# One transpose of q in place of two, earlier loads of q and k, and PV five steps behind its scores in place of seven

## The chip, the cores and the metric

The kernel runs on one core of a Trainium2 chip. The metric is the device time of one launch in microseconds (us). Each comparison was run in rounds beside the kernel before, on the same chip. A run over 1.5% above the fastest of its kernel counts as slow.

## The reference

Eight batches of eight heads, 576 positions, head size 64; then two matrix products with a leaky ReLU between them.

```python
scores = q @ k.T / 8                                 # per batch and head
thresh = scores.max(-1) - tau
scores = where(scores >= thresh, scores, -1e9)
attn   = softmax(scores)
x      = (attn @ v) -> [4608, 512]                   # heads side by side
h      = x @ w_in                                    # [4608, 2048]
out    = maximum(0.01 * h, h) @ w_out                # [4608, 512]
```

## The kernel before

The kernel is one loop over 144 **steps**, 18 per batch. A step takes 128 rows of q for a pair of heads. It makes scores (`sc`) on TensorE, copies them with their maximum on VectorE (`sf`), subtracts (`P`), and takes the exponential on ScalarE (`w`). Two steps make a **unit** (the last units, in the final batch, have one). A unit's weights `w` are transposed by one DMA into `wt`, and later TensorE multiplies them by v ("PV"). Finished groups of rows give "h units" and "o units" of the two matrix products, one pair of them a step.

For the next batch, each half (two pairs of heads) of k and q is loaded in fp32 (`km`, `qm`), split in two fp16 parts (`ks`, `qs`) on ScalarE and GpSimd, and transposed by DMA (`kst`, `qst`; a **turn** in the code).

SyncE issues, in one in-order queue, all loads of q and k, all transposes and all stores. GpSimd issues the loads of v and of the weights.

```python
LAG = 7                       # steps from a unit's last scores to its PV
PREP = (3, 9)                 # first step of preparing each half of the next batch
...
def turn(nm, b, hb, g=None):  # DMA transposes
    t = turned(nm, b, hb); s_ = split_tile(nm, b, hb)
    if nm == "k":
        nc.sync.dma_start(out=t..., in_=s_..., transpose=True)          # 128 rows
    else:
        nc.sync.dma_start(out=t[:, g]..., in_=s_[ds(64 * g, 64)]..., transpose=True)   # 64 rows
...
for b in range(1, B):
    s0 = 18 * (b - 1)
    for hb in range(2):
        t0 = s0 + (PREP1 if b < 2 else PREP)[hb]
        at(t0 - 4, load k half);  at(t0 - 3, load q half)
        at(t0 - 1, fp16 of k);    at(t0 + 1, fp16 of q)      # ScalarE
        ...
        at(t0 + 4, turn k)
        for g in range(2):
            at(t0 + 7 + g, turn q of pair g)
    for i in range(4):
        at(18 * b + i, load_v(b, i))
```

Units that end in step 130 or later, close to the end, have a lag of four steps in both kernels. Within a step, TensorE's order is scores, then o and h units, then PV. SyncE's order is stores, then the `wt` transpose of the unit that ended two steps earlier, then the loads and turns above.

## Time and profile before

| | before |
|---|---|
| median of three runs | 538.18 us (536.41 to 541.07) |
| profiled span | 537.4 us |
| first `sf` / last step's first `sf` to the end | at 12.8 us / 45.8 us |
| batches 1 to 6, mean of one (from its first `sf` to the next batch's) | 60.8 us |

In the profile PE is TensorE and PEld its weight loads, DVE is VectorE, ACT ScalarE, POOL GpSimd, and SP SyncE (SPq: it issues a DMA). The **granted clock** is the share of TensorE's full clock rate that it got. The profile names a group by line, engine and operation, with "output<-input" by the program's names. The waits view gives total us, how often, and the longest. A batch of 18 undisturbed steps, 3.12 us each by the starts of `sf`, would take 56.2 us.

### The profile page before, as it was taken

The numbers are of one execution on the slowest core, as the hardware profiler recorded it, in microseconds if no ns is written. First come the engines' busy times: TensorE is split into PE (matmuls) and PEld (weight loads), VectorE is DVE, ScalarE is ACT, GpSimd is POOL, SyncE is SP. The second block draws the span as 40 slices with busy tenths as digits, with TensorE's granted clock in tenths as the row PEclk, the third lists the DMA queues.
The fourth block names the chain that finished last, engine by engine and source line by source line (L and its number), as shares of the span: only waits on it lengthen the run. The fifth ranks groups of instructions, "written<-read, shape, count | busy, mean of one in ns | idle before, by whom it ended". The sixth has DMA issues, their size and how long they took to land.

```text
span 537.4 us, 13446 instructions
## 1 busy us (share of the span) xinstructions
PE 476.8 (89%) x4912; PEld 294.3 (55%) x4912; DVE 463.8 (86%) x1213; ACT 421.8 (78%) x924; POOL 278.2 (52%) x476
## 2 busy tenths in 40 slices
PE   5655885999989997999998995999999998999996
PEld 3323553655655664666654663566555665566673
DVE  4976895999999996999997995999999999999542
ACT  6785894998799886898897884898799888778331
POOL 5475843675477634574576643675466643222000
PEclk9758797999999997999998998899999999999999
DMA  8999999999999999999999999999999999976401
GB/s 269 207 189 236 158 183 250 222 189 183 208 221 224 166 195 263 222 176 192 227 184 205 153 199 245 241 189 172 219 199 241 182 166 188 189 125 122 96 25 59
DMA packets 279617, 101.79 MB, mean 189 GB/s; under 512 B 254464, under 2 KB 266752, under 8 KB 279552
## 3 DMA queue, kind: packets, MB, share of 16 engines
q1 hardware_dynamic: 266496, 92.03, 90.9%
q0 software_dynamic: 13056, 8.92, 12.5%
q8 instruction: 38, 0.62, 0.5%
q14 instruction: 27, 0.22, 0.2%
HBM read 36.70 MB, written 9.44 MB: 86 GB/s over the span
## 4 chain that ended last, share of the span: by engine, by line
DVE 41%; PE 15%; issue 15%; DMA 13%; POOL 7%; ACT 6%; SPq 2%; POOLq 0%; DVEq 0%; ACTq 0%
DVE sf L398 16%; DMA km<-in_k_dram 8%; DVE gT L223 7%; DVE P L554 7%; PE op L243 6%; PE hp L243 5%; DMA wt<-w 4%; DVE w L544 4%; POOL P L525 3%; PE sc L338 3%; DVE osb L279 3%; DVE xT L379 2%; SPq L179 2%; ACT P L524 2%; ACT gT L257 1%
## 5 line engine op out<-in xcount | busy, mean ns | idle before, releaser
L398 DVE TENSOR_SCALAR_CACHE_REDUCE sf<-sc 128x576 f32<-128x576 f32 x288 | 205.0, 747 | 8.3 <-PE sc L338 7.5
L559 ACT ACTIVATE w<-P 128x576 f16<-128x576 f16 x288 | 193.7, 674 | 7.9 <-DVE P L554 3.8
L243 PE MATMUL op<-wout,gT 128*128 128x512 f16 x576 | 150.9, 386 | 13.5 <-DVE osb L279 13.1
L243 PE MATMUL hp<-xT,win 128*128 128x256 f16 (+1 forms) x1344 | 153.9, 261 | 5.5 <-DVE gT L223 3.9
L338 PE MATMUL sc<-kst,qst 64*128 64x320 f16 (+1 forms) x1536 | 137.8, 299 | 18.6 <-DVE sf L398 17.8
L243 PEld LDWEIGHTS <-win 128*128 128x128 f16 x1344 | 118.4, 99 | 50.7 <-issue 10.0
L524 ACT ACTIVATE P<-sf,bb 128x576 f16<-128x576 f32 x144 | 111.1, 771 | 43.6 <-POOL bb L523 39.2
L223 DVE SCALAR_TENSOR_TENSOR gT<-hp,gT 128x512 f16<-128x512 f32 x144 | 98.3, 683 | 35.5 <-ACT gT L257 35.5
L338 PEld LDWEIGHTS <-qst 64*128 64x128 f16 x1536 | 75.9, 98 | 70.7 <-issue 51.2
L525 POOL TENSOR_SCALAR P<-sf,bb 128x576 f16<-128x576 f32 x139 | 105.8, 761 | 14.1
L257 ACT ACTIVATE gT<-hp 128x512 f16<-128x512 f32 x144 | 83.6, 580 | 18.9 <-PE hp L243 18.9
L243 PEld LDWEIGHTS <-gT 128*128 128x128 f16 x576 | 46.4, 98 | 76.2 <-issue 40.7
L523 POOL TENSOR_SCALAR bb<-mx 128x2 f32<-128x2 f32 x139 | 27.3, 196 | 107.0 <-DVE sf L398 95.3
L554 DVE TENSOR_SCALAR P<-P 128x1152 int16<-128x1152 int16 x144 | 81.7, 568 | 0.0
L369 PE MATMUL pv<-wt,v 128*64 128x256 f16 (+2 forms) x1000 | 55.9, 251 | 11.5 <-DMA wt<-w 11.0
L559 ACT ACTIVATION_READ_ACCUMULATOR w<-P 128x1 f32 x288 | 54.3, 188 | 0.0
L369 PEld LDWEIGHTS <-v 128*64 128x64 f16 x1000 | 37.6, 111 | 27.6 <-issue 23.6
L149 ACT ACTIVATE ks<-km 128x640 f16<-128x640 f32 (+1 forms) x32 | 20.0, 672 | 34.6 <-DMA km<-in_k_dram 34.6
L159 POOL TENSOR_TENSOR ks<-km,ks 128x320 f16<-128x320 f32 (+1 forms) x56 | 39.8, 732 | 11.3 <-DVE P L554 11.3
L159 POOL TENSOR_TENSOR qs<-qm,qs 128x576 f16<-128x576 f32 x28 | 35.8, 1280 | 13.6 <-DVE P L554 13.6
L544 DVE TENSOR_SCALAR w<-rc 128x256 f16<-128x256 f32 (+1 forms) x76 | 39.9, 525 | 2.6
L379 DVE TENSOR_TENSOR xT<-pv,wt 128x128 f16<-128x128 f32 x128 | 31.6, 290 | 6.4 <-PE pv L369 6.3
(35 smaller groups left out, 211.8 us busy)
## 6 DMA issues: line engine op xcount, KB each, us to landing
km<-in_k_dram SPq DMA_DIRECT2D x16, 576.0 KB, 5.5
qm<-in_q_dram SPq DMA_DIRECT2D x16, 576.0 KB, 6.0
out_dram<-osb SPq DMA_DIRECT2D x36, 256.0 KB, 3.7
v<-in_v_dram POOLq DMA_DIRECT2D x16, 160.0 KB, 5.5
v<-in_v_dram POOLq DMA_DIRECT2D x16, 128.0 KB, 5.6
win<-in_moe_w_in_dram POOLq DMA_DIRECT2D x8, 256.0 KB, 10.3
wout<-in_moe_w_out_dram POOLq DMA_DIRECT2D x8, 256.0 KB, 11.8
wt<-w SPq DMA_TRANSPOSE x76, 6.3
```

Of the source, the lines that this page charges most:

```text
L159: return nc.gpsimd.tensor_tensor(out=dst[:, h], in0=src[:, h], in1=h_[:, h], op=AX.subtract)
L223: nc.vector.scalar_tensor_tensor(out=G.g[u], in0=hp, scalar=0.01, in1=G.g[u], op0=AX.mult, op1=AX.add)
L243: nc.tensor.matmul(out=out_, lhsT=lhsT, rhs=rhs, start=start, stop=stop, skip_group_check=True)
L257: nc.scalar.activation(out=G.g[u], in_=hp, func=AF.Relu, bias=0.0, scale=0.99)
L338: nc.tensor.matmul(out=sc[h][:, cols], lhsT=qt[r, g, qi, ds(2 * c, 2), :].rearrange("p t r -> p (t r)"), rhs=rhs, start=(i == 0), stop=(i ...
L369: nc.tensor.matmul(out=o_[ds(64 * h, 64)], lhsT=vt[:, pp, h, j, :], rhs=w_[:, :, 4 * h + j, :], start=(j == 0), stop=(j == 4), skip_group_ ...
L398: nc.vector.tensor_scalar(out=sf, in0=sc[h][:, ds(SC0, 576)], scalar1=C, scalar2=None, op0=AX.mult, op1=AX.max, accum_out=mx[:, h : h + 1])
L524: nc.scalar.activation(out=P_[:, 1, :], in_=sB, func=AF.Identity, bias=bb[:, 1:2], scale=1.0)
L525: (nc.vector if s < SPOOL else nc.gpsimd).tensor_scalar(out=P_[:, 0, :], in0=sa, scalar1=1.0, scalar2=bb[:, 0:1], op0=AX.mult, op1=AX.add)
L544: nc.vector.tensor_scalar(out=W_[:, :, 1152:1280].rearrange("p i (h r) -> p i h r", h=2), in0=rc[:, 0:nw, :].unsqueeze(3).to_broadcast([12 ...
L554: anchor[0] = nc.vector.tensor_scalar(out=pi, in0=pi, scalar1=NEG, scalar2=None, op0=AX.max)
L559: nc.scalar.activation(out=uW[ui][:, i, ds(576 * h, 576)], in_=P_[:, h, :], func=AF.Exp, bias=exp_bias, scale=1.0, accum_out=usm[ui][:, i, ...
```

## The change

The intent: issue one 128-row transpose of q for two pairs instead of two of 64 rows, by loading q with the two pairs in alternating partitions. Issue the loads of q and k earlier, so that ScalarE no longer waits for them. Take PV sooner, so that the h and o units start sooner.

```diff
-    LAG = 7
+    LAG = 5
+    LOADS = (-4, 3)
@@ load_half
+        if nm == "km":
+            nc.sync.dma_start(out=m, in_=in_.rearrange("f p h x -> (f p) h x"))
+        else:
+            for f in range(2):
+                nc.sync.dma_start(out=m.rearrange("(p f) h x -> f p h x", f=2)[f], in_=in_[f])
@@ turn: one transpose of 128 rows for q as for k
@@ scores: the weights of a pair are every second column
-    lhsT=qt[r, g, qi, ds(2 * c, 2), :].rearrange("p t r -> p (t r)"),
+    lhsT=qt[r, qi, ds(2 * c, 2)].rearrange("d t a b -> d (t a b)")[:, g::2],
@@ schedule
-            at(t0 - 4, ... load_half(k, ...))
-            at(t0 - 3, ... load_half(q, ...))
+            at(s0 + LOADS[hb], ... load_half(k, ...))
+            at(s0 + LOADS[hb] + 1, ... load_half(q, ...))
-            for g in range(2):
-                at(t0 + 7 + g, ... turn("q", b, hb, g))
+            at(t0 + 7, ... turn("q", b, hb))
```

Counted in steps of the batch in which the work is done (from 0; 18 is step 0 of the next batch), the first half's loads move from 17 and 18 to 14 and 15, and the second half's from 5 and 6 to 3 and 4.

## The prediction

> **What bounds the kernel now.** I read the page first, then the waits, then the instruction timeline around the longest wait, then windows of steps with and without a stall. The page (busy us, share, count; then DMA queues with packets, MB and share of 16 engines):
>
> ```profile
> PE 476.8 (89%) x4912; PEld 294.3 (55%) x4912; DVE 463.8 (86%) x1213; ACT 421.8 (78%) x924; POOL 278.2 (52%) x476
> ...
> q1 hardware_dynamic: 266496, 92.03, 90.9%
> q0 software_dynamic: 13056, 8.92, 12.5%
> ```
>
> Three engines and the DMA queues are all close to full, so no single busy share names the bound. The windows (length, then busy time per engine, granted clock, DMA share, GB/s) separate the two states:
>
> ```profile
> 160.00:200.00 40.00, 39.56 (x427) 25.15 (x426) 39.79 (x105) 35.52 (x81) 24.10 (x41) 1.00 1.10 197
> ...
> 324.00:345.00 21.00, 15.04 (x157) 8.88 (x157) 13.88 (x36) 13.03 (x30) 9.68 (x18) 0.84 1.14 237
> ```
>
> In an undisturbed stretch TensorE and VectorE are both busy over 98% of the time: they bound the step. There are 144 steps (288 of the maximum instructions `sf`, two a step); in undisturbed stretches the starts of `sf` are 3.0 and 3.2 or 3.3 us apart in turn, mean 3.12. So 144 x 3.12 = 449 us is the steady work, where first `sf` to end of steps takes about 482 (from 12.8 to some 494). The 33 us between are stalls like 324 to 345, where every engine drops, and the clock with them. The waits (total, times, longest) say which:
>
> ```profile
> DVE gT L223 <- ACT gT L257: 35.5, 20, 6.7
> ACT ks L149 <- DMA km<-in_k_dram: 34.6, 9, 7.5
> ...
> PE pv L369 <- DMA wt<-w: 11.0, 7, 4.7
> ```
>
> VectorE waits for ScalarE, which stands in front of the fp16 copy of k (`ks`) because the load of `km` has not landed. The timeline at the longest one, of the DMA-issuing queue and then of ScalarE (start, length):
>
> ```profile
> 75.22 5.40 SPq L548 DMA_TRANSPOSE wt<-w  x1
> 80.67 1.49 SPq L179 DMA_TRANSPOSE qst<-qs  x1
> 82.20 1.34 SPq L96 DMA_DIRECT2D km<-in_k_dram  x1
> ```
> ```profile
> 87.98 1.25 ACT L149 ACTIVATE ks<-km 128x640 f16<-128x640 f32 x2 [7.47 <-DMA km<-in_k_dram]
> ```
>
> The load is programmed three steps ahead of its use, some 9.4 us, and needs 5.7 us to land. But it stands in one in-order queue behind a `wt` transpose that took 5.40 us and a q transpose, so it is issued only when ScalarE is already waiting. Of the step distances, the excess over 3.12 at the steps with k's copy is 6.8, 1.7, 3.8, 0.6, 2.5, 6.1 and 1.1, and 3 to 4 more in the step or two after: **about 26 us of load stalls**. The first batch has one other stall, 4.75 us, for its first `wt`.
>
> **What the Trainium skill says.**
> - "DMA: Bandwidth & Descriptors", section "Rules for kernel authors": two transfers to disjoint partition halves are not worth it, they serialize; use one of 128 partitions. The trace agrees for transposes. Windows in which only a 64-row q transpose moved data, then one with only a 128-row k transpose (last column GB/s):
>
> ```profile
> 114.50:116.50 2.00, 2.00 (x17) 1.11 (x14) 2.00 (x5) 2.00 (x6) 1.41 (x3) 1.00 0.94 135
> 120.80:122.60 1.80, 1.80 (x18) 0.87 (x16) 1.80 (x5) 1.22 (x4) 1.21 (x2) 1.00 0.97 139
> 107.80:109.80 2.00, 2.00 (x18) 1.11 (x14) 2.00 (x5) 2.00 (x6) 1.41 (x2) 1.00 1.16 218
> ```
>  The same sentence speaks against the new split of the q load in two; no run here shows that yet.
> - "Advanced Engine Details and Errata", section "X-Bar Transpose (TRN2)", expects 350 to 400 GB/s of transposes. This trace shows 218 and less; I use the trace.
> - "TensorE: Matmul & The Clock Gate", section "Weight-path perf modes — Fast Weight Load (FWL) and DoubleRow": the fast load needs 128 columns and allows a column step of up to 1,024 elements, so step 2 should keep it. The trace has 92/94/148 ns (min, median, max) for 64x128 weights of q and 102/107/107 for 64x64, so 128 columns are indeed not dearer; it has no weights with a step.
>
> **The change part by part.**
> *One q transpose.* 28 transposes of 288 KB become 14 of 576 KB. At 137 GB/s two halves hold the path for 2 x 288 KB = 590 kB / 137 = 4.3 us; at 218 one takes 2.7. Saved: 1.6 us per half batch, 3.2 per batch, some 22 us of DMA time in all, none of it directly on the path. Issue time does not fall: 2 x 1.37 us against k's 3.05 for the same size. The q loads double from 16 to 32 issues of half the size, at about 0.4 us each; in the built program issues per batch stay at 2 + 2 + 2 + 4 + 9 + 4 or 5, as before. The order of instructions shows the same 1,536 + 384 weight loads of q and the same matmuls; GpSimd's list is unchanged, and only six copies in the first two steps change their pattern.
>
> *Loads further ahead.* The first half's k goes from one step before the batch's own 18 steps of preparation to four before, the second half's from step 5 to step 3. Lead before use: 6 and 5 steps (19 and 16 us) instead of 3 (9.4). Needed: 5.7 us to land plus up to 6.5 in the queue (75.22 to 82.20 is 7.0). Both fit, and the batch's end no longer has two q transposes, two loads and the v loads in one place. Worth nearly the 26 us; I take **25**.
>
> *PV five steps behind.* No work is added or removed. (a) The h and o units run one pair a step and start when the first group's PV is done, two steps sooner, so two pairs fewer are left for the end, where TensorE is alone; in the chain, units there follow at 1.76 us (517.33, 519.09, 520.85). Gain 3.5. (b) The first PV: its `wt` is issued at 25.0 and lands at 41.9, in the weight loads' traffic, and nothing of that changes. Before, TensorE reached it in step 8 and waited 4.75 us:
>
> ```profile
> 42.02 1.36 PE L369 MATMUL pv<-wt,v 128*64 128x256 f16 x10 [4.75 <-DMA wt<-w]
> ```
>  Now it gets there in step 6, about 6 us sooner, and waits about 10.7. Loss 6, less 1 where steps were light: 5. Ends together: **+1.5**. (c) In the batches, the weights are ready on VectorE and ScalarE some 15.7 us before PV's result is taken (172.85 to 188.45 for one unit); two steps less leaves 15.7 - 6.2 = 9.5, and minus 1 for PV itself `wt` must land within **8.4 us** of being ready. In the trace this time is 5.1 to 7.6 where the queue had just drained (332 to 376 us) and 9 to 15.7 where it was behind (262 to 330). So the backlog must shrink by several us, or PV waits. The q transposes give back 3.2 per batch, the loads no longer sit in the burst; I expect 0 to 2 us of PV waits in most batches, on average **0.6 x 7 = 4**.
>
> Sum: 538.2 - 25 + 1.5 + 4 = **519 us**.
>
> **The rivals.** *PV's wait takes the place of the load's.* For it: from 262 to 333 us the queue was never empty, serving 22 steps' transposes in 71.7 us, 3.26 a step, slower than the engines' 3.12; the stalls were what let it drain. A slack of 8.4 us is little above the 5.1 of an empty queue. Against: 3.2 us less per batch is 0.18 a step, so about 3.08. If so, 2 to 3 us per batch in place of 0.6, total 529 to 533. *The strided weights load slower.* TensorE is full: 12 loads a step at, say, twice 94 ns would add up to 1.1 us a step and make it slower, 560 and more. Against: the step allowed by the page. I give it 4%. *The DMA was not the limit at all*, and the later PV costs nothing: then 512 to 515. *The split q load lands late*: it has 5 or 6 steps, so hidden.
>
> **Range and chances.** Upper end 533 from the first rival, lower 506 if the first `wt` also lands sooner and steps shorten slightly. 2% lies at 527.4, inside the first rival's half of the range. **Faster** 0.72, **within 2%** 0.24, **slower** 0.04.
>
> **What would show it.** Right: ScalarE's wait for `km` falls from 34.6 us to under 8 (4 of it at the very start); 14 q transposes, with some 218 GB/s when alone; `sf` 3.0 to 3.3 apart at the steps with k's copy; weight loads of q still near 94 ns; the first PV waits about 10 us; the stretch after the last step is 3 to 4 us shorter. Wrong if TensorE's wait for `wt` in mid-kernel exceeds 10 us in total (first rival), if q's weight loads grow, or if the km wait only moves.

## The result, and the profile after

| | before | changed |
|---|---|---|
| median | 539.03 us (536.41 to 541.07, 4 runs) | 559.68 us (555.97 to 560.72, 4 runs) |
| profiled span | 537.4 us | 557.4 us |
| ScalarE waits for `km` | 34.6 us | 2.4 us |
| TensorE waits for `wt` | 11.0 us | 49.6 us |
| batch 0 (first `sf` to batch 1's) | 57.2 us | 64.2 us |
| batches 1 to 6, mean of one | 60.8 us | 63.7 us |
| last step's first `sf` to the end | 45.8 us | 41.5 us |

The ratio is 1.037, with a 95% interval of 1.031 to 1.044: **slower**. A ratio here is the mean time of one kernel's fast runs over that of the other's fast runs of the same rounds, so it is not quite the ratio of the medians.

The page of the changed kernel, engines and DMA queues:

```profile
PE 480.1 (86%) x4912; PEld 297.5 (53%) x4912; DVE 463.1 (83%) x1213; ACT 424.4 (76%) x924; POOL 278.4 (50%) x476
...
q1 hardware_dynamic: 266304, 92.03, 85.7%
q0 software_dynamic: 13056, 8.92, 12.1%
```

The work is the same: busy times of TensorE and VectorE are within 4 us of before, and the bytes are equal. Only the share of busy time fell. The waits of the changed kernel:

```profile
PE pv L362 <- DMA wt<-w: 49.6, 18, 10.6
...
DVE xT L372 <- PE pv L362: 40.3, 15, 10.1
...
ACT ks L154 <- DMA km<-in_k_dram: 2.4, 1, 2.4
```

The load's wait is gone, as intended. TensorE's wait for `wt` stands in its place, and it is larger. In the windows (length, busy time per engine, granted clock, DMA share, GB/s), a stretch with such a stall, the part of it up to the end of TensorE's wait, the part after that, and an undisturbed stretch:

```profile
138.00:160.00 22.00, 13.86 (x113) 8.24 (x112) 13.88 (x37) 12.86 (x30) 6.30 (x13) 0.84 0.99 167
138.00:153.60 15.60, 7.46 (x70) 4.82 (x70) 9.57 (x24) 10.87 (x25) 4.75 (x9) 0.94 1.17 201
156.00:159.00 3.00, 3.00 (x22) 1.66 (x20) 2.81 (x8) 1.09 (x2) 0.94 (x2) 0.57 0.07 14
...
165.00:195.00 30.00, 28.74 (x307) 18.13 (x303) 28.92 (x77) 27.03 (x60) 21.22 (x35) 1.00 1.06 213
```

All engines drop together, and over the stall the DMA moves less too (167 GB/s against 213). It moves less not while TensorE waits (201 GB/s up to 153.6 us) but just after: from 156 to 159 us the DMA has almost nothing to carry (14 GB/s), because no unit's weights became ready between 145.86 and 158.87 us. TensorE works again there, at a granted clock of 0.57, so the stall also slowed what came right after it; this part is small, since TensorE's busy time grew by 3.3 us in all.

The stall comes in the same place of nearly every batch. SyncE's timeline around it:

```profile
129.56 2.73 SPq L176 DMA_TRANSPOSE kst<-ks  x1
132.34 0.58 SPq L100 DMA_DIRECT2D km<-in_k_dram  x1
133.10 4.94 SPq L540 DMA_TRANSPOSE wt<-w  x1
138.09 1.36 SPq L103 DMA_DIRECT2D qm<-in_q_dram  x2
139.54 4.07 SPq L176 DMA_TRANSPOSE qst<-qs  x1
143.72 0.60 SPq L273 DMA_DIRECT2D out_dram<-osb  x1
144.49 18.67 SPq L540 DMA_TRANSPOSE wt<-w  x3
```

The weights of the unit whose `wt` opens the last line were ready at 138.07 us (the end of VectorE's last write to `w`). SyncE came to them at 144.49, after two q loads, the q transpose and a store; they landed at 153.25, 15.2 us after being ready. TensorE, in its own timeline, had been waiting for 5.91 us:

```profile
153.29 1.28 PE L362 MATMUL pv<-wt,v 128*64 128x256 f16 x10 [5.91 <-DMA wt<-w]
```

The q transpose itself was not waiting for its data. GpSimd had written the last part of `qs` at 133.49:

```profile
132.21 1.28 POOL L164 TENSOR_TENSOR qs<-qm,qs 128x576 f16<-128x576 f32 x1 [0.59 <-DVE P L546]
```

So the delay was queueing. The same holds elsewhere: from 70 to 440 us of this trace, SyncE went on to every load and every turn of q and k within 0.3 us of its previous issue, so none of them held up the queue by waiting for data or a buffer. For reading the experiments I use this time, **ready to landed**, worked out for every unit from the same records. With lag five it has to stay under about 8.4 us, by the prediction's own working.

### The profile page after: what moved, and what is told of

Read it like the earlier page. It is cut to its first block, busy times and chain, and to the rows that moved or that the text cites. A ratio compares the mean times of both kernels' runs of the same rounds, so it can differ in the third digit from the quotient of the medians.

```text
span 557.4 us, 13439 instructions
## 1 busy us (share of the span) xinstructions
PE 480.1 (86%) x4912; PEld 297.5 (53%) x4912; DVE 463.1 (83%) x1213; ACT 424.4 (76%) x924; POOL 278.4 (50%) x476
## 3 DMA queue, kind: packets, MB, share of 16 engines
q1 hardware_dynamic: 266304, 92.03, 85.7%
## 4 chain that ended last, share of the span: by engine, by line
DVE 40%; DMA 20%; PE 19%; issue 11%; POOL 6%; ACT 2%; POOLq 0%; SPq 0%; DVEq 0%; ACTq 0%
DMA wt<-w 19%; DVE sf L391 17%; DVE gT L216 7%; DVE P L546 6%; PE sc L331 5%; PE op L236 5%; PE hp L236 4%; DVE w L536 4%; PE pv L362 4%; POOL P L517 3%; DVE osb L272 2%; DVE xT L372 2%; POOL qs L164 2%; POOL bb L515 1%; ACT w L551 1%
## 5 line engine op out<-in xcount | busy, mean ns | idle before, releaser
L391 DVE TENSOR_SCALAR_CACHE_REDUCE sf<-sc 128x576 f32<-128x576 f32 x288 | 205.2, 748 | 18.4 <-PE sc L331 18.2
L236 PE MATMUL op<-wout,gT 128*128 128x512 f16 x576 | 152.7, 390 | 1.9 <-DVE osb L272 1.7
L331 PE MATMUL sc<-kst,qst 64*128 64x320 f16 (+1 forms) x1536 | 135.8, 302 | 14.2 <-DVE sf L391 13.6
L331 PEld LDWEIGHTS <-qst 64*128 64x128 f16 x1536 | 74.3, 98 | 64.7 <-issue 44.3
L362 PE MATMUL pv<-wt,v 128*64 128x256 f16 (+2 forms) x1000 | 58.5, 257 | 49.9 <-DMA wt<-w 49.6
L250 ACT ACTIVATE gT<-hp 128x512 f16<-128x512 f32 x144 | 83.6, 581 | 19.5 <-PE hp L236 19.5
L546 DVE TENSOR_SCALAR P<-P 128x1152 int16<-128x1152 int16 x144 | 79.7, 553 | 0.0
L362 PEld LDWEIGHTS <-v 128*64 128x64 f16 x1000 | 40.8, 113 | 65.7 <-issue 63.8
L126 POOL DMA_DIRECT2D v<-in_v_dram x32 | 20.6, 643 | 23.6 <-DVE P L546 8.6
```

What stands on the lines that cost most here:

```text
L236: nc.tensor.matmul(out=out_, lhsT=lhsT, rhs=rhs, start=start, stop=stop, skip_group_check=True)
L250: nc.scalar.activation(out=G.g[u], in_=hp, func=AF.Relu, bias=0.0, scale=0.99)
L331: nc.tensor.matmul(out=sc[h][:, cols], lhsT=qt[r, qi, ds(2 * c, 2)].rearrange("d t a b -> d (t a b)")[:, g::2], rhs=rhs, start=(i == 0), s ...
L362: nc.tensor.matmul(out=o_[ds(64 * h, 64)], lhsT=vt[:, pp, h, j, :], rhs=w_[:, :, 4 * h + j, :], start=(j == 0), stop=(j == 4), skip_group_ ...
L391: nc.vector.tensor_scalar(out=sf, in0=sc[h][:, ds(SC0, 576)], scalar1=C, scalar2=None, op0=AX.mult, op1=AX.max, accum_out=mx[:, h : h + 1])
L546: anchor[0] = nc.vector.tensor_scalar(out=pi, in0=pi, scalar1=NEG, scalar2=None, op0=AX.max)
```

## The experiments

**Theory A**, after the comparison: the shorter lag alone makes the loss. **Rivals**: the SyncE queue of transposes and loads is so full that any wait removed returns as another (B); the merged transpose or the split load costs by itself (C). Later rivals are named where they came up.

### The parts alone

`all_lag7` is the changed kernel with the lag undone; the other three are the kernel before with one part each.

```diff
all_lag7:    -    LAG = 5                          +    LAG = 7
lag5_only:   -    LAG = 7                          +    LAG = 5
loads_only:  -    at(t0 - 4, ...load k)            +    at(s0 + LOADS[hb], ...load k)      # q one step later
q_only:      the change without LOADS and with LAG = 7
```

> The changed kernel with PV again seven steps behind. Theory A (the shorter lag alone makes the loss: the time from ready weights to landed wt reaches 12 to 15 us at one unit of each batch, and five steps leave about 8.4): the wait for wt in the batches falls from 39 us to under 6, the wait for the km load stays under 4, total 512 to 520 us. Theory B (the transposes queue is over its capacity once the load stalls, which let it drain, are gone): wt waits of 20 us or more stay and grow along the kernel, total 530 to 545. Theory C (the merged q transpose or the split load costs by itself): over 540.

> The kernel before, with only the loads moved ahead (two q transposes, unsplit q load, lag seven). Theory A: the km wait falls from 34.6 us to under 4; lag seven covers most of the queue, though the two half-rate q transposes leave it longer; total 514 to 524. Theory B: wt waits take the place of the load waits, total 530 to 540. If the loads are worth what I predicted (25 us) and the q transpose nothing, this equals all_lag7.

> The kernel before, with only the merged q transpose and its split q load (loads where they were, lag seven). Theory A: the queue is shorter by some 1.6 us per half batch, so the km load is issued a few us sooner and its waits fall from 34.6 to 15 to 25 us; total 524 to 535. Theory C (merging or splitting costs): 540 or more, with km waits as long or longer.

> The kernel before, with only PV five steps behind. Theory A: waits for wt appear (30 us or more in the batches, 10.7 at the first), and they push the use of km back so that part of the load waits go; total 550 to 570. Theory B (saturated queue, the lag does not matter since one wait replaces another): 538 to 546.

| kernel | median us | ratio to before (95%) | batches 1 to 6, mean us | waits for `km` / `wt` / turned q, us |
|---|---|---|---|---|
| `all_lag7` | 535.28 | 0.997 (0.990 to 1.005) | 60.1 | 4.9 / 18.4 / 8.6 |
| `loads_only` | 536.78 | 0.998 (0.992 to 1.004) | 60.3 | 5.6 / 28.2 / 1.3 |
| `q_only` | 528.78 | 0.984 (0.975 to 0.992) | 58.8 | 21.0 / 6.6 / none |
| `lag5_only` | 562.95 | 1.044 (1.037 to 1.051) | 63.7 | 12.6 / 56.0 / none |

The waits include some 2.4 us for the first `km` and, for the first `wt`, 4.5 to 5.9 us at lag seven or 9.8 to 11.2 at lag five.

The shorter lag alone costs all of the loss and more: this half of theory A holds, and rival B's expectation for it (538 to 546 us, the lag does not matter) fell. The other half of A fell: with the lag undone, the kernel does not reach 512 to 520 us. `loads_only` shows why, in two lines of its waits:

```profile
PE pv L370 <- DMA wt<-w: 28.2, 12, 6.7
...
ACT ks L150 <- DMA km<-in_k_dram: 5.6, 2, 3.3
```

The load's wait went from 34.6 to 5.6 us, and the wait for `wt` rose from 11.0 to 28.2. Moving the loads bought nothing, as rival B says. Rival C fell: the merged q transpose (with the split load that it needs) is the only part that gains; its interval lies below 1, though a gain of 2% is not certain. It is the only part that shortens the transfers. It even shortens the `km` wait (34.6 to 21.0), though no load was moved.

### How the lag acts

```diff
all_lag6:    -    LAG = 5   +    LAG = 6
all_lag9:    -    LAG = 5   +    LAG = 9
q_lag5:      the changed kernel with the loads back at t0 - 4 and t0 - 3
```

> The changed kernel with PV six steps behind. If the loss is the part of wt's time that the slack does not cover, each step of lag is worth up to 3.1 us per batch until the slack passes 12 to 15 us: total about halfway, 544 to 552, wt waits in the batches 15 to 28 us. If the queue's capacity were all that counts, it would equal all_lag7 (535).

> The changed kernel with PV nine steps behind: 21 us of slack for wt instead of 8.4. Theory F (a bunch of transfers that a longer slack can cover): no wt waits in the batches, only waits for the turned q of 1 to 2 us per batch stay, a batch takes 56 to 57.5 us, less 2 to 4 us given back at the end; total 522 to 530. Theory E (the queue is over capacity): a batch still takes 59 to 60 us, some other wait takes the place, total 534 to 542.

> The changed kernel with the loads back where they were (merged q transpose, lag five). Theory F (moved ahead, the loads stand in the queue between the k turn of step 13 and the q turn of step 16, just ahead of the wt of step 17, and make it late): the unit ready in step 17 lands 8 to 10 us after being ready instead of 12 to 15, wt waits in the batches fall from 39 to about 20 us, total 542 to 550. Theory E (only the sum of the transfers counts, wherever the loads stand): 553 to 560, like the changed kernel.

| kernel | median us | ratio (95%) | batches 1 to 6, mean us | waits for `km` / `wt` / turned q, us |
|---|---|---|---|---|
| changed (lag 5) | 559.68 | 1.037 (1.031 to 1.044) | 63.7 | 2.4 / 49.6 / none |
| `all_lag6` | 536.77 | 0.998 (0.991 to 1.005) | 60.6 | 2.4 / 27.2 / none |
| `all_lag7` | 535.28 | 0.997 (0.990 to 1.005) | 60.1 | 4.9 / 18.4 / 8.6 |
| `all_lag9` | 534.42 | 0.991 (0.985 to 0.997) | 59.7 | 4.7 / 3.8 / 20.2 |
| `q_lag5` | 555.22 | 1.030 (1.025 to 1.036) | 62.6 | 4.2 / 46.2 / none |

From five steps to six a batch gains 3.1 us, just one step; I had expected about half of the way, and it was all of it. Beyond six there is almost nothing: `all_lag6` and `all_lag7` cannot be told apart, as `all_lag6`'s other alternative, that only the queue's capacity counts, had it. At nine steps `wt` is nearly never late, and a third consumer of the same queue waits instead, TensorE's scores for the turned q:

```profile
PEld L331 <- DMA qst<-qs: 21.8, 6, 8.1
PE sc L331 <- DMA qst<-qs: 20.2, 5, 7.8
```

A batch still takes 59.7 us. So theory F's hope for `all_lag9` (522 to 530 us) fell, and the queue's view held (534 to 542). SyncE was issuing nearly all the time there: its pauses of over 0.3 us between issues add up to 3.4 us in batches 1 to 6, so it was not held up by a `wt` buffer that the later PV still needed. `q_lag5` fell for F likewise: with the loads out of the way, the unit ready in step 17 landed in 7 to 10 us, as F expected, but then the next unit took 11 to 14 and TensorE waited there.

### What fills the queue at lag five

Four edits of the changed kernel take something away from the place of the stall, or move it.

```diff
all_vearly:        -  at(18 * b + i, load_v)       +  at(18 * b - 10 + i, load_v)
all_light_loads:   +  if b > 1: m, in_ = m[:, :, 0:64], in_[:, :, :, 0:64]      # fixed tiles, wrong result
all_light_vearly:  both
all_no_turns:      +  if b < 2:  (before both turns; scores read batch 1's q and k, wrong result)
all_turn_late:     -  at(t0 + 7, turn q)           +  at(t0 + 8, turn q)
```

> The changed kernel (lag five), each batch's v loaded ten steps sooner, away from the end of the batch. In the changed kernel the wt of the unit ready in step 17 lands 12 to 15 us after its weights were ready, while v's packets interleave with the transposes. Theory D (v's traffic is what slows the transposes there): that time falls to 6 to 9 us, the wt waits in the batches fall from 39 us to under 15, total 530 to 542. Theory E (the k, q and wt transfers of the burst alone fill the queue; v only lengthens it a little): wt waits of 25 us or more stay, total 550 or more.

> The changed kernel (lag five), but from batch 2 on each q and k load brings only 64 of 576 columns, so the results are wrong on purpose: same issues, a ninth of the bytes; 4.2 MB fewer per batch pair. Theory E or F alike (the loads' bytes in the queue delay wt): wt waits in the batches fall from 39 us to 10 to 20, total 530 to 542. Rival G (the in-order issue on SyncE, not the bytes, makes wt late): little change, 552 or more.

> all_light_loads (wrong on purpose) with v also ten steps sooner, lag five. Theory H (loads of k and q and v interleaved with the transposes make wt late): wt waits in the batches under 10 us, total 522 to 532. Theory I (the k and q transposes ahead of wt in the queue make it late): 20 us or more stay, total 538 to 546.

> The changed kernel (lag five) without the k and q transposes of batches 2 to 7 (scores use batch 1's, results wrong on purpose); all loads and v stay. Theory H: wt waits of 25 us or more stay, total 545 or more. Theory I: they fall under 10 us, total 520 to 532.

> The changed kernel (lag five) with each q transpose one step later, so issued behind the wt of that step instead of ahead of it. If the place in the queue is the cause: the wt ready in step 17 lands in 8 to 10 us instead of 12 to 15, wt waits in the batches fall from 39 to under 20 us, total 537 to 547. If the amount of transposes in the burst is the cause: the wait moves to the next unit's wt, waits stay above 30 us, total 552 to 560.

The two columns on the right are worked out from the traces: the ready-to-landed time of the unit ready in step 17, in batches 1 to 5, and in how many of 54 units of batches 1 to 6 SyncE began within 0.2 us of readiness, that is, had no queue.

| kernel | median us | ratio (95%) | waits for `wt`, us | ready to landed, us | no queue |
|---|---|---|---|---|---|
| before (lag 7) | 539.03 | 1 | 11.0 | 8.4 to 13.6 | 8 |
| changed | 559.68 | 1.037 (1.031 to 1.044) | 49.6 | 11.5 to 15.2 | 25 |
| `all_vearly` | 555.26 | 1.031 (1.023 to 1.040) | 56.2 | 10.3 to 12.3 | 17 |
| `all_light_loads` | 544.74 | 1.013 (1.009 to 1.017) | 39.2 | 10.0 to 13.1 | 25 |
| `all_light_vearly` | 539.29 | 1.004 (0.998 to 1.010) | 39.5 | 6.7 to 9.8 | 22 |
| `all_no_turns` | 519.25 | 0.967 (0.960 to 0.974) | 19.8 | 5.8 to 7.5 | 50 |
| `all_turn_late` | 549.65 | 1.013 (0.998 to 1.028) | see below | | |

Moving v did not help: theory D fell (here, and in the three runs at lag seven below). Taking away eight ninths of the load bytes from batch 2 on saved 15 us of time but left 29 of the 39 us of `wt` waits in the batches, between the two expectations (the loads' bytes, and SyncE's mere issue, rival G). Both together still left 28 us in the batches (39.5 less 11.2 for the first), in other units: theory H (the loads alone) fell. Taking away the k and q transposes settled it for theory I (519.25 us, just below its range). SyncE's timeline of `all_no_turns` at the same place in a batch:

```profile
187.06 3.69 SPq L541 DMA_TRANSPOSE wt<-w  x1
190.80 1.36 SPq L103 DMA_DIRECT2D qm<-in_q_dram  x2
192.26 0.59 SPq L273 DMA_DIRECT2D out_dram<-osb  x1
193.36 9.43 SPq L541 DMA_TRANSPOSE wt<-w  x2
```

and its wait for `wt`, of which 10.2 us are the first PV and 4.5 the one batch before which turns still happened:

```profile
PE pv L362 <- DMA wt<-w: 19.8, 8, 10.2
```

All loads, v and stores are still there and the lag is five, yet batches 2 to 6 take 56.1 to 58.2 us, next to the 56.2 of undisturbed steps. The changed kernel had no waits for the turned q or k, so the gain is not theirs. At lag five, then, it is the k and q transposes that make `wt` late. The loads add to it (15 us); that v does is not shown.

`all_turn_late` asked whether the place in the queue is enough. It is **inconclusive**: two of its four runs, the profiled one among them, were slow, and the interval is 3% wide. All its runs (541.64 to 552.18 us) lie below every run of the changed kernel (555.97 to 560.72), which were made in another session, so the order may be worth something; its slow profile cannot say how.

What stays open is which part of that queue is the limit. SyncE spends 2.4 to 3.1 us to issue an undisturbed transpose of 576 or 640 KB, and at 215 GB/s the DMA engines need 2.7 to 3.0 us to move it; no run here separates the two. One number speaks for the moving: in `q_only` the issues of a half batch's q took longer than before (2.74 + 2 x 0.64 us against 2 x 1.37 + 0.47, medians), and yet a batch took 2.0 us less.

### Better versions

```diff
q_vearly:                q_only with v at 18 * b - 10 + i
all_lag7_vearly:         all_lag7 with v at 18 * b - 10 + i
before_vearly:           the kernel before with v at 18 * b - 10 + i
all_lag7_spread:         all_lag7 with LOADS = (-7, 3)
all_lag7_spread_vearly:  both
q_vearly_turn_late:      q_vearly with the q transpose at t0 + 8
```

> As q_only (loads where they were, lag seven), with v ten steps sooner. Theory D: the km load and the transposes ahead of it pass faster, km waits fall from 21 us to under 12, total 512 to 522. Theory E: 525 to 532. Near all_lag7_vearly if loads further ahead are worth nothing once the burst is gone.

> As all_lag7, with v ten steps sooner. Theory D: the remaining waits for wt (13 us in the batches) and for the turned q (8 us) go, total 510 to 520. Theory E: little change, 528 to 536.

> The kernel before, with v ten steps sooner and nothing else. Theory D: km waits fall from 34.6 us to 10 to 20, total 518 to 530. Theory E: within 1% of before.

> As all_lag7, with the first half's loads in steps 11 and 12, between the q turn of step 10 and the k turn of step 13, in place of steps 14 and 15. Theory F: the wt ready in step 17 lands in 10 to 13 us instead of 15 to 19, wt and q waits fall from 22 us in the batches to under 10, total 520 to 528. Theory E: 530 to 537.

> Candidate for a better kernel: merged q transpose, loads of the first half in steps 11 and 12, v ten steps sooner, lag seven. If the gains of the spread loads (1.2% over all_lag7) and of v (0.6%) add: 522 to 527. If the queue's mean load per batch sets the time, no better than q_vearly (525.7): 525 to 532.

> q_vearly with each q transpose one step later. Lag seven already covers the queue there; the q transpose now stands just ahead of the km load in step 17, so km waits stay near 22 us or grow: 524 to 534.

| kernel | median us | ratio (95%) | batches 1 to 6, mean us |
|---|---|---|---|
| `q_vearly` | 525.73 | 0.977 (0.971 to 0.983) | 58.2 |
| `q_vearly_turn_late` | 526.80 | 0.980 (0.972 to 0.989) | 58.2 |
| `all_lag7_spread_vearly` | 527.94 | 0.982 (0.976 to 0.989) | 58.7 |
| `all_lag7_spread` | 528.66 | 0.981 (0.974 to 0.987) | 59.4 |
| `all_lag7_vearly` | 532.27 | 0.992 (0.983 to 1.000) | 59.5 |
| `before_vearly` | 537.80 | 0.999 (0.992 to 1.006) | 60.4 |

The correct kernel with the lowest median is `q_vearly`: the merged q transpose with the old loads and lag, and earlier v. It beats the kernel before by 2.3% (interval 1.7 to 2.9%) and, by way of it, the changed one by some 6%; its interval overlaps those of `q_only` and of the three kernels below it in the table, so that v's move itself gains is not shown. Loads placed between a q transpose and a k transpose (`all_lag7_spread`) did better than loads placed between a k and a q transpose (`all_lag7`), 0.981 against 0.997, but no better than loads left alone. Why is open: theory F expected the `wt` of step 17 to land within 10 to 13 us there, and it took 15.1 to 16.5. The gains of placing and of v did not add (527.94 us). In `q_vearly`, `all_lag7_vearly` and `before_vearly` theory E's ranges held and D's fell. No correct kernel here got the mean of batches 1 to 6 under 58 us.

## Why the prediction was wrong, by its own steps

The measured terms come from the two traces.

| part | predicted, us | measured, us |
|---|---|---|
| first PV, batch 0 | +5 | +7.0 (57.2 to 64.2) |
| loads further ahead, and PV's waits in the batches | -25 + 4 = -21 | +17.4 in batches 1 to 6 (6 x 2.9), -0.6 in batch 7 |
| end (last `sf` to the end of the span) | -3.5 | -4.3 |
| start | 0 | +0.3 |
| **sum** | **-19.5** | **+19.8** (spans: +20.0) |

The waits behind the second row: for `km` 34.6 to 2.4 us, for `wt` in the batches 6.3 to 39. One at a time, and per batch, the merged transpose gave -2.0 us, the loads -0.5 and the lag +2.9; together +2.9, so the parts do not add.

- **What bounds the kernel now.** The reading of the stalls was right in place and wrong in kind. ScalarE did wait for `km`, and I charged "about 26 us of load stalls" to the load. They were the place where a full queue happened to show. When the load no longer waits, `wt` does (`loads_only`), or the turned q (`all_lag9`), and a batch takes 59.7 to 60.3 us in place of 60.8. The line that should have warned me was in the prediction itself, and I miscounted it: from 261.77 to 333.50 us SyncE issued the `wt` of ten units, 20 steps and not 22, so 3.59 us a step and not 3.26. Less the 0.18 that the q transposes give back, that is still 3.41, above the engines' 3.12; the 3.08 with which I argued against the first rival came from this slip.
- **"One q transpose ... none of it directly on the path."** The transfer got shorter as I said, but "none of it directly on the path" was wrong. Alone, the 128-row q transpose moved 215 GB/s (below), and the 3.2 us of queue time per batch that I worked out bought 2.0 us of the batch (60.8 to 58.8, `q_only`): most of it was on the path. The strided weights cost nothing, as expected (94 ns median before and after).

```profile
184.30:185.20 0.90, 0.90 (x11) 0.41 (x6) 0.90 (x2) 0.90 (x2) 0.50 (x1) 1.00 1.17 215
```
```profile
L331 PEld LDWEIGHTS <-qst x1536: 92/94/148, 10.7 to 515.0; 64*128 64x128 f16 x192
```

- **"Loads further ahead ... I take 25."** This step failed. The lead was enough (waits fell to 2.4 us), but the time was not saved: `loads_only` gained 0.2%, within its error (0.5 us a batch where I had taken about 3.6). On top of the merged transpose, the moved loads look like a cost: 528.78 to 535.28 us at lag seven, 555.22 to 559.68 at lag five, though the intervals overlap each time.
- **"PV five steps behind", (a) and (b).** Right in mechanism, near in size. The end is 4.3 us shorter (3.5 predicted). The first PV waited 10.57 us (10.7 predicted); batch 0 lost 7.0 where I took 5.

```profile
42.14 1.36 PE L362 MATMUL pv<-wt,v 128*64 128x256 f16 x10 [10.57 <-DMA wt<-w]
```

- **"(c) ... on average 0.6 x 7 = 4."** This step failed most. The bound of 8.4 us was a fair one, and two units a batch overran it: 11.5 to 15.2 us for the one ready in step 17, and 9.8 to 13.4 for the next. I wrote that "the loads no longer sit in the burst". They still did: they moved from behind that `wt` to ahead of it, between the k and the q transpose. The first rival, "PV's wait takes the place of the load's", was the right story. It was sized at 2 to 3 us per batch on top of the -25 of the loads (3 would give 536 us, not the 533 that I wrote). The lag alone measured +2.9 per batch (`lag5_only`), and the loads gave nothing back to set against it.
- **Why a shorter lag costs more than the waits it replaces.** At lag seven the queue works while the engines do, and most units (46 of 54 before) found it occupied. At lag five TensorE stops for the one late unit; then no weights are made, the queue runs dry (25 of 54 units found it empty, against 8) and the time is lost to it. The 85.7% of the hardware DMA queue, against 90.9%, is that loss seen on the page. In SyncE's own record, its pauses of over 0.3 us between issues add up to 13.0 us in batches 1 to 6 before and to 51.3 in the changed kernel. That the slope between five and six steps is one step per batch fits it. But at lag six the pauses are 26.1 us and the time is that of lag seven (6.0 us), so idle time does not turn into lost time one for one. This is argued from the counts; no experiment held the queue full at lag five.

## What to carry to other kernels

When several consumers wait on one in-order DMA queue that is nearly full, the one that is seen waiting need not be the cause. Here moving its transfer only passed the wait to the next one, and shortening a transfer in the queue gained. Before shortening a pipeline's lag, list for every unit the time from "ready" to "landed", and compare the lag with the longest in a burst, not with the mean. A slack that looks idle may be what lets a queue work through its burst.

## What the Trainium skill lacked or had wrong

- "Advanced Engine Details and Errata", section "X-Bar Transpose (TRN2)", expects 350 to 400 GB/s. These runs show 215 to 218 for a 128-row transpose with the DMA to itself.
- "DMA: Bandwidth & Descriptors", section "Rules for kernel authors", advises against two transfers to partition halves because they serialize. For transposes the runs show more than that: a 64-row transpose also moved only 135 to 139 GB/s, and merging two of them, with the split load, took 1.6% off the kernel (`q_only`). For plain loads, the split (here in alternate partitions, not halves) cost issue time: two issues of 637 ns (median) where one took 468 ns.
- No page gives the time on this chip for which a transpose holds the queue that issues it (the DMA page has only sequencer cycles, for "previous generations"): here 2.4 to 3.1 us for 576 or 640 KB undisturbed, during which nothing behind it was issued.
